# Attention and token selection on one core: ranking by half sections, the gate's exp moved, one group's q scaled through TensorE

## The chip, the cores and the metric

One core of a Trainium2 chip runs the whole program. The metric is the device time of one execution in microseconds (us). All arithmetic is float32. The engines are TensorE (PE; its weight loads are shown as PEld), VectorE (DVE), ScalarE (ACT) and GpSimd (POOL); SyncE (SP) only issues DMAs.

## What is computed

Eight batches of twelve heads go through attention (448 positions, 64 columns per head) with normalized q and k. Its result, 448 tokens of 768 columns per batch, then goes through a layer that only the 128 best tokens of a batch get:

```python
q_n, k_n = rmsnorm(q, g_q), rmsnorm(k, g_k)        # x / sqrt(mean(x*x) + 1e-6) * g
attn = softmax(q_n @ k_n.T / sqrt(64))
x = concat_heads(attn @ v)                         # (8, 448, 768)
scores = x @ w_gate                                # one number per token
top = the 128 tokens of a batch with the highest scores
x[top] += sigmoid(scores[top]) * (relu(x[top] @ w1) @ w2)    # 768 -> 1024 -> 768
```

## The kernel before, in words

**Units and groups.** Four heads of a batch make a group, so there are 24 groups, three to a batch. A group has seven units, one for each 64 keys: 168 units. `scores(u)` (L265) multiplies one block of keys with all queries into two of the four score banks (pool `ps_sc`), and ACT's Exp turns them into probabilities `p` (seven buffers). `values(u)` multiplies `p` with v, `add_probs(u)` sums the probabilities on DVE. After a group's seventh unit, `values_out`, `sum_keys`, `invert_sums` and `to_tokens` (twice) bring the result into the token rows `x` of the batch, divided by the softmax sums.

**Normalization.** For each group, tokens are loaded (`load_tok`), squared on ACT (`squares`), summed on DVE and raised to -1/2 on POOL (`sum_squares`, L201). The factors of k go into the Exp as its scale. Those of q must lie along the free axis: `rows_out` writes them to DRAM, `rows_in` reads them back spread over the partitions (`bc`), and `scale_q` (L235) multiplies q by them on DVE. For group 0 alone `scale_q_early` (L239) does the same without DRAM: 28 small matmuls (the trace shows each matmul as two) in two score banks, and two multiplications on DVE.

**Ranking and selection.** When a batch's third group is done, `gate` gives the scores (DVE), `spread` copies them along the free axis, `score_rows` transposes them on PE and copies the result out on ACT, `count` compares each score with all others (four DVE instructions, L431), `annotate` makes the rank, the sigmoid (an Exp on ACT, L452, and six small DVE instructions) and the row number, `select` scatters the chosen rows into a DRAM buffer by four indirect DMAs on POOL (L464), and `load_selected` (L482, SP queue) reads them back. `mixture` is the two layers for the 128 rows: six transposes (L498), then eight pieces of PE work.

**Order.** It is written out by hand, each engine runs its instructions in that order, and semaphores are the only waits. The loop at the end (L698) goes by sections `q` of four units: scores and values of the units, then two half sections. A half section runs the actions whose slot it is (`at(slot, ...)`; a slot is a unit number, so section q has the slots 4q to 4q+3), one piece of a `mixture` (`piece`), and one waiting task (`opening(q, place)`, place 0 before the halves, 1 and 2 after the first and the second). `tasks` is a first-in first-out list, and only its first entry is looked at. `last_tokens` (L620) puts `gate`, `store_x` and `spread` into the next section and `ranks_of` as a task after it; `ranks_of` (L633) puts `count`, `annotate` and `select` into the section after that, and `load_selected` five slots behind `select`. `ready[b]` is the first section in which `mixture(b)` may begin, and `first_ff(b)` its lower bound. After the last unit (section 42) the loop goes on until the last batches are through. `mixture` works in one bank (`moe`), and only the last batch's uses the score banks (`bank()`, L511). A helper tile `aux` has one bank too, or the `moe` bank where no mixture is running.

Of the kernel before, what the change touches and what calls it, by code (L numbers as in the profile page):

```python
# [26 lines left out]
def fast(  # L27
# [25 lines left out]
    nc = tc.nc  # L53
# [52 lines left out]
    def load_q(n):  # L106
        c = n % NG * 2
        load("qT", qTs, qT[n // NG, c : c + 2].rearrange("c p s -> p c s"), [128, 2, S], n, 3)
# [10 lines left out]
    load_tok(0, 0)  # L119
    load_tok(0, 1)  # L120
    load_q(0)
    load_k(0)
    load_tok(1, 0)
    load_tok(1, 1)
    load_v(0)
    load_q(1)
# [250 lines left out]

    gates, rowss, highers, ranks, slots_dram = {}, {}, {}, {}, {}  # L380

    def store_x(b):
        nc.sync.dma_start(
# [21 lines left out]
    def spread(b):  # L405
# [5 lines left out]
        nc.vector.tensor_copy(out=t, in_=sc[:, :, None].to_broadcast([CP, NJ, CP]))  # L411
        rowss[b] = t

    def score_rows(b):
        t = rowss[b]
        ps = aux([128, 512], "row_ps")
        for j in range(NJ):
            nc.tensor.transpose(
                out=ps[:CP, CP * j : CP * (j + 1)], in_=t[:, j, :], identity=ident[:CP, :CP]
            )  # L420
        rows = moe_pool.tile([CP, S], F32, name="score_rows")
        nc.scalar.copy(out=rows, in_=ps[:CP, 0:S])
        rowss[b] = rows

    def count(b, js):
# [14 lines left out]

    def annotate(b):

        sc, x = gates.pop(b), xs[b]
        ranks[b] = moe_pool.tile([CP, NJ], I32, name="rank", bufs=2)
        nc.vector.tensor_copy(out=ranks[b], in_=highers.pop(b))

        parts = moe_pool.tile([CP, 2, NJ], F32, name="parts")
        nc.vector.tensor_scalar_min(out=parts[:, 0], in0=sc, scalar1=0.0)
        nc.vector.tensor_scalar(
            out=parts[:, 1], in0=sc, scalar1=0.0, scalar2=-1.0, op0=OP.max, op1=OP.mult  # L450
        )
        nc.scalar.activation(out=parts, in_=parts, func=AF.Exp)  # L452
        nc.vector.tensor_add(out=parts[:, 1], in0=parts[:, 0], in1=parts[:, 1])
        nc.vector.reciprocal(out=parts[:, 1], in_=parts[:, 1])
        nc.vector.tensor_mul(out=x[:, :, DM], in0=parts[:, 0], in1=parts[:, 1])
        nc.vector.tensor_scalar_add(out=x[:, :, DM + 1], in0=token_f, scalar1=float(b * S))  # L456

    def select(b):
# [26 lines left out]
    def mixture(b):  # L485

        n = CAP
        xe = xes.pop(b)
        xeT = moe_pool.tile([128, NDC, 128], F32, name="xeT")
        half = NDC // 2  # L490
        for a in range(2):
            if a == 0:
                ps = ps_moe.tile([128, 512], F32, tag="moe", name="moe_ps")
            else:
                ps = aux([128, 512], "xeT_ps")
            for i in range(half):
                dc = half * a + i
                nc.tensor.transpose(  # L498
                    out=ps[:, 128 * i : 128 * i + n],
                    in_=xe[:n, 128 * dc : 128 * (dc + 1)],  # L500
                    identity=ident[:n, :n],
                )
            nc.scalar.copy(  # L503
                out=xeT[:, half * a : half * (a + 1), :n],
                in_=ps[:, : half * 128].rearrange("p (i t) -> p i t", t=128)[:, :, :n],
            )
        row = moe_pool.tile([128, 1], I32, name="row", bufs=2)
        nc.vector.tensor_copy(out=row[:n], in_=xe[:n, DM + 1 : DM + 2])
        yield False

        def bank():  # L511

            if b == B - 1:
                return ps_sc.tile([128, 512], F32, name="sc")
            return ps_moe.tile([128, 512], F32, tag="moe", name="moe_ps")

        hT = moe_pool.tile([128, NFC, 128], F32, name="hT")
        for f0 in range(0, NFC, 4):
            ps = bank()
            for i in range(4):  # L520
# [15 lines left out]
            yield True  # L536
        for a in range(2):
            cols = slice(DM // 2 * a, DM // 2 * (a + 1))
            ps = bank()
            for fc in range(NFC):  # L540
                nc.tensor.matmul(  # L541
                    out=ps[:n, : DM // 2],
                    lhsT=hT[:, fc, :n],
                    rhs=w2[:, fc, cols],
                    start=(fc == 0),
                    stop=(fc == NFC - 1),
                )
                if fc == NFC // 2 - 1:
                    yield False
            nc.vector.scalar_tensor_tensor(  # L550
                out=xe[:n, cols],
                in0=ps[:n, : DM // 2],
                scalar=xe[:n, DM : DM + 1],
                in1=xe[:n, cols],
                op0=OP.mult,
                op1=OP.add,
            )
            if a == 1:
                nc.gpsimd.indirect_dma_start(  # L559
                    out=out.flatten_outer_dims(),  # L560
                    out_offset=bass.IndirectOffsetOnAxis(ap=row[:n, :1], axis=0),
                    in_=xe[:n, 0:DM],
                    in_offset=None,
                )
            yield True
# [11 lines left out]
    def at(slot, fn, *args):  # L577
        todo.setdefault(slot, []).append(lambda: fn(*args))

    def task(when, fn, *args):  # L580
        tasks.append((when, lambda: fn(*args)))

    def opening(q, place):
        if tasks and tasks[0][0] <= (q, place):
            tasks.pop(0)[1]()

    def prepare(n, slot):
        sq = {}
# [6 lines left out]
    for n in range(1, n_groups):  # L595
        s0 = NI * n
        if n > 2:
            at(max(s0 - 24, 0), load_tok, n, 0)
            at(max(s0 - 24, 0), load_tok, n, 1)
        at(max(s0 - 4, 3), scale_q, n)  # L600
        if n > 1:
            prepare(n, max(s0 - 16, 0))
            at(max(s0 - 13, 2), load_q, n)
            at(max(s0 - 11, 2), load_k, n)
            at(max(s0 - 11, 2), load_v, n)
# [9 lines left out]
        task((q + 1, 0), to_tokens, n, 0)  # L615
        task((q + 1, 1), last_tokens, n)

    now = [0]

    def last_tokens(n):  # L620
        to_tokens(n, 1)
        b, g = divmod(n, NG)
        q = now[0]

        s = PER * (q + 1) if n < n_groups - 1 else -9
        at(s, gate, n)
        if g < NG - 1:
            return
        at(s, store_x, b)
        at(s + 1, spread, b)  # L630
        task((q + 1, 1) if n < n_groups - 1 else (q + 1, 0), ranks_of, b)

    def ranks_of(b):  # L633
        score_rows(b)
        s = PER * (now[0] + 1) if b < B - 1 else -9
        at(s, count, b, (0, 1))
        at(s + 1, count, b, (2, 3))
        at(s + 2, annotate, b)
        at(s + 2, select, b)
        at(s + 7 if b < B - 1 else s + 3, load_selected, b)  # L640
        if b < B - 1:
            ready[b] = max(now[0] + 4, first_ff(b))
        else:
            ready[b] = 0

    def first_ff(b):


        return (units + 4 - NG * NI * (B - 2 - b)) // PER

    def run_values(upto, q):
        ended = False
# [10 lines left out]
            add_probs(u)  # L663

    sq = {}
    sq[0, 0] = squares(0, 0)
    sum_squares(0, 0, sq.pop((0, 0)))
    sq[0, 1] = squares(0, 1)
    sum_squares(0, 1, sq.pop((0, 1)))
    sq[1, 0] = squares(1, 0)  # L670
    sq[1, 1] = squares(1, 1)
    scale_q_early(0)
    sum_squares(1, 0, sq.pop((1, 0)))
    load_tok(2, 0)
    load_tok(2, 1)
    rows_out(1)
    sum_squares(1, 1, sq.pop((1, 1)))
    rows_in(1)

    def run(slots):  # L680
        for slot in sorted(x for x in todo if x < 0 or x in slots):
# [14 lines left out]
    waiting = list(range(units))  # L696
    moe, ready, done, q = iter(()), {}, 0, 0
    while done < B or tasks:  # L698
        now[0] = q
        k = PER * q  # L700
        for half in range(HALVES):
            for u in (k + 2 * half, k + 2 * half + 1):
                if u < units:
                    scores(u)
            run_values(k + 2 * half - 1, q)
        opening(q, 0)
        for half in range(HALVES):
            run((k + 2 * half, k + 2 * half + 1))
            end = piece(q)
            spare[0] = end is None and half == 0  # L710
            if end is not None or half == 0 or not ready:
                opening(q, half + 1)
            spare[0] = False
            run(())
        q += 1
# [531 lines left out]
```

## Time and profile before

| | |
|---|---|
| median of 3 runs | 570.66 us (570.5 to 572.22) |
| profiled execution | 572.16 us |
| its span | 570.4 us (1.76 us lie around it) |
| PE busy | 515.3 us, 90% |
| DVE busy | 354.7 us, 62% |
| ACT busy | 278.3 us, 49% |
| POOL busy | 196.6 us, 34% |
| mean granted PE clock | 0.972 |

Busy times are of the span. A granted clock of 1.00 is the 2.4 GHz level and 0.50 the 1.2 GHz level; a stretch in between is a mixture of both. The timeline view gives instructions in order of time, like ones merged, with the engine's idle time before them and what ended it.

### The profile page before, as it was taken

Reading aid. Unit: us, or ns where it says so; the run is one execution under the profiler, and the core shown is the slowest. Engines: PE = TensorE matmul, PEld = TensorE weight load, DVE = VectorE, ACT = ScalarE, POOL = GpSimd, SP = SyncE. Lnnn points to the kernel's source line nnn. Section 1 sums busy time; section 2 is a strip of 40 time slices with the busy share of each in tenths; the row PEclk is TensorE's granted clock in tenths of the full one; section 3 lists DMA queues with packets and bytes.
Section 4 is the critical chain, followed back from the end, with each engine's and each line's share of the span. In section 5 each row is a group of like instructions: output and inputs, shape, how many; then the busy total and the mean of one; then the engine's idle time right before and its main releaser. Section 6 shows DMA issues by size and latency. Waiting matters only on the chain. (4 is left out here: it accounts for less than half of the span.)

```text
span 570.4 us, 16312 instructions
## 1 busy us (share of the span) xinstructions
PE 515.3 (90%) x7028; PEld 288.5 (51%) x7028; DVE 354.7 (62%) x699; ACT 278.3 (49%) x506; POOL 196.6 (34%) x100
## 2 busy tenths in 40 slices
PE   6789787989997998999899999999999999929895
PEld 6334332347542456544664475446644665418482
DVE  2497887784768757578577556676596637472000
ACT  2757664665444755447464444474646454401010
POOL 3654643751232532173152332640354200130200
PEclk9979997999999899999999999999999999968999
DMA  6696889875762754619835682638816320012100
GB/s 227 206 305 197 290 240 346 289 234 173 224 217 75 214 167 166 194 31 271 269 81 174 191 243 83 163 117 247 219 52 186 99 99 2 30 58 96 56 29 32
DMA packets 47108, 94.02 MB, mean 165 GB/s; under 512 B 11702, under 2 KB 29878, under 8 KB 47028
## 3 DMA queue, kind: packets, MB, share of 16 engines
q1 hardware_dynamic: 43684, 86.58, 49.1%
q0 software_dynamic: 3200, 6.31, 3.2%
q8 instruction: 57, 0.93, 0.7%
q14 instruction: 23, 0.19, 0.1%
q10 hardware_dynamic: 144, 0.00, 0.0%
HBM read 75.39 MB, written 25.36 MB: 177 GB/s over the span
## 5 line engine op out<-in xcount | busy, mean ns | idle before, releaser
L285 ACT ACTIVATE p<-sc,rinv 128x448 f32<-128x448 f32 x336 | 186.2, 639 | 105.4 <-PE sc L276 87.3
L201 POOL TENSOR_TENSOR rinv<-ss,neg_half 128x14 f32<-128x14 f32 x48 | 142.9, 2981 | 218.3 <-issue 102.8
L276 PE MATMUL sc<-qT,kT 64*32 64x448 f32 x2688 | 155.4, 553 | 13.4 <-ACT p L285 7.1
L302 PE MATMUL av<-p,v 64*32 64x448 f32 x2688 | 151.6, 547 | 0.0
L315 DVE TENSOR_TENSOR sum<-sum,p 128x896 f32<-128x896 f32 x120 | 130.3, 1086 | 21.6 <-ACT p L285 14.1
L302 PEld LDWEIGHTS av<-p,v 64*32 64x32 f32 x2688 | 56.4, 109 | 74.3 <-issue 67.1
L276 PEld LDWEIGHTS sc<-qT,kT 64*32 64x32 f32 x2688 | 49.2, 108 | 85.8 <-issue 54.1
L522 PE MATMUL moe_ps<-xeT,w 128*128 128x128 f32 x672 | 80.7, 278 | 0.3 <-ACT hT L531 0.3
L522 PEld LDWEIGHTS moe_ps<-xeT,w 128*128 128x128 f32 x672 | 77.8, 194 | 3.7 <-issue 2.9
L541 PE MATMUL moe_ps<-w,hT 128*128 128x384 f32 x224 | 77.8, 492 | 1.4 <-DVE xe L550 0.7
L197 DVE TENSOR_REDUCE ss<-sq 128x14 f32<-128x896 f32 x48 | 51.8, 1078 | 11.3 <-ACT sq L191 10.9
L464 POOL DMA_INDIRECT selected<-x,rank x32 | 36.0, 1125 | 64.6 <-DVE x L456 56.7
L371 DVE TENSOR_TENSOR x<-x_ps,rden 112x512 f32<-112x512 f32 x48 | 32.8, 687 | 37.4 <-PE x_ps L369 37.2
L541 PEld LDWEIGHTS moe_ps<-w,hT 128*128 128x128 f32 x224 | 40.5, 190 | 30.1 <-issue 2.2
L191 ACT ACTIVATE sq<-tok 128x896 f32<-128x896 f32 x48 | 45.2, 962 | 5.8 <-DMA tok<-in_tok_dram 5.8
L395 DVE SCALAR_TENSOR_TENSOR prod<-x,wg 112x256 f32<-112x256 f32 x96 | 40.4, 421 | 2.5
L559 POOL DMA_INDIRECT out_dram<-xe,row x8 | 12.3, 1533 | 82.0 <-DVE rden L357 46.4
L531 ACT ACTIVATE hT<-moe_ps 128x512 f32<-128x512 f32 x14 | 8.4, 597 | 48.1 <-PE moe_ps L522 48.1
L357 DVE RECIPROCAL rden<-denT_ps 112x16 f32<-112x16 f32 x24 | 6.1, 254 | 40.1 <-PE denT_ps L355 40.0
L369 PEld LDWEIGHTS x_ps<-ident,xT 128*112 128x112 f32 x192 | 21.9, 137 | 17.8 <-issue 11.6
L369 PE MATMUL x_ps<-ident,xT 128*112 128x128 f32 x192 | 29.1, 284 | 2.0 <-ACT xeT L503 1.1
L550 DVE SCALAR_TENSOR_TENSOR xe<-moe_ps,xe 128x384 f32<-128x384 f32 x14 | 8.6, 616 | 35.6 <-PE moe_ps L541 35.6
(63 smaller groups left out, 281.3 us busy)
## 6 DMA issues: line engine op xcount, KB each, us to landing
tok<-in_tok_dram SPq DMA_DIRECT2D x48, 448.0 KB, 7.0
qT<-in_qT_dram SPq DMA_DIRECT2D x24, 448.0 KB, 5.7
kT<-in_kT_dram SPq DMA_DIRECT2D x24, 448.0 KB, 5.0
v<-in_vp_dram SPq DMA_DIRECT2D x24, 448.0 KB, 6.0
out_dram<-x SPq DMA_DIRECT2D x8, 1344.0 KB, 7.1
bc<-rows SPq DMA_DIRECT2D x46, 224.0 KB, 5.9
xe<-selected SPq DMA_DIRECT2D x8, 385.0 KB, 3.4
w<-in_moe_w_dram SPq DMA_DIRECT2D x6, 512.0 KB, 10.1
```

The source lines that it names most:

```text
L191: nc.scalar.activation(out=sq, in_=t, func=AF.Square, scale=scale)
L197: nc.vector.tensor_reduce(out=ss, in_=sq, axis=AX.X, op=OP.add)
L201: nc.gpsimd.tensor_tensor(out=rinv.rearrange(flat), in0=ss.rearrange(flat), in1=neg_half.to_broadcast([128, 2 * NI]), op=OP.pow,)
L276: nc.tensor.matmul(out=scs[hh][o : o + 32, 0:S], lhsT=kTs[n][r, c, D * i + k0 : D * i + k0 + 32], rhs=qTs[n][r, c, :], start=True, stop=True,)
L285: nc.scalar.activation(out=p[:, hh], in_=scs[hh][:, 0:S], func=AF.Exp, scale=rinvs[n, 1][:, hh, i : i + 1],)
L302: nc.tensor.matmul(out=avs[n][c][o : o + 32, 0:S], lhsT=vs[n][r, hh, i, d0 : d0 + 32], rhs=probs[u][r, hh], start=(i == 0), stop=(i == NI ...
L315: nc.vector.tensor_tensor(out=sums[n], in0=probs[u - 1] if i == 1 else sums[n], in1=probs[u], op=OP.add)
L369: nc.tensor.transpose(out=ps[:CP, j, :], in_=t[:, j, :], identity=ident)
L395: nc.vector.scalar_tensor_tensor(out=prod, in0=xs[b][:, j, cols], scalar=1.0, in1=wg[:, cols], op0=OP.mult, op1=OP.mult, accum_out=gates[b ...
L464: w = nc.gpsimd.indirect_dma_start(out=t[:, :], out_offset=bass.IndirectOffsetOnAxis(ap=rank[:, j : j + 1], axis=0), in_=x[:, j, :], in_of ...
L522: nc.tensor.matmul(out=ps[:, 128 * i : 128 * i + n], lhsT=w1[:, dc, 128 * (f0 + i) : 128 * (f0 + i + 1)], rhs=xeT[:, dc, :n], start=(dc == 0),
L541: nc.tensor.matmul(out=ps[:n, : DM // 2], lhsT=hT[:, fc, :n], rhs=w2[:, fc, cols], start=(fc == 0), stop=(fc == NFC - 1),)
```

## The change

Five things, and some order at the start:

- `last_tokens` and `ranks_of` put their actions into the current or next half section (`soon`) and no longer into the next section; `ranks_of` becomes the first of the tasks, `opening` looks at the first two, `load_selected` comes four slots behind `select`, and `ready` and `first_ff` move one section forward.
- The sigmoid's two inputs are made in `spread` and its Exp runs on ACT right behind the copy in `score_rows`; `annotate` keeps the three DVE instructions that follow.
- Group 1's q is scaled by `scale_q_early` too, as the first task of section 0, without `rows_out(1)` and `rows_in(1)`.
- `mixture` of any batch takes score banks from section 43 on.
- At the start `load_tok(1, 0)` is issued ahead of `load_k(0)`, and `sum_squares(1, 0)` comes ahead of `scale_q_early(0)`.

```diff
-    load_k(0)
     load_tok(1, 0)
+    load_k(0)
...
     def spread(b):
...
+        parts[b] = moe_pool.tile([CP, 2, NJ], F32, name="parts", bufs=2)
+        nc.vector.tensor_scalar_min(out=parts[b][:, 0], in0=sc, scalar1=0.0)
+        nc.vector.tensor_scalar(
+            out=parts[b][:, 1], in0=sc, scalar1=0.0, scalar2=-1.0, op0=OP.max, op1=OP.mult
+        )
     def score_rows(b):
...
         nc.scalar.copy(out=rows, in_=ps[:CP, 0:S])
+        nc.scalar.activation(out=parts[b], in_=parts[b], func=AF.Exp)
     def annotate(b):
-        parts = moe_pool.tile([CP, 2, NJ], F32, name="parts")
-        nc.vector.tensor_scalar_min(out=parts[:, 0], in0=sc, scalar1=0.0)
...
-        nc.scalar.activation(out=parts, in_=parts, func=AF.Exp)
...
         def bank():
-            if b == B - 1:
+            if PER * now[0] >= units + 2:
                 return ps_sc.tile([128, 512], F32, name="sc")
...
     def opening(q, place):
-        if tasks and tasks[0][0] <= (q, place):
-            tasks.pop(0)[1]()
+        now[:] = q, place
+        for i, (when, fn) in enumerate(tasks[:2]):
+            if when <= (q, place):
+                tasks.pop(i)
+                fn()
+                return
...
-        at(max(s0 - 4, 3), scale_q, n)
         if n > 1:
+            at(s0 - 4, scale_q, n)
...
+    def soon():
+        q, place = now
+        return PER * q + 2 * place if PER * q < units else -9
     def last_tokens(n):
         to_tokens(n, 1)
         b, g = divmod(n, NG)
-        q = now[0]
-        s = PER * (q + 1) if n < n_groups - 1 else -9
+        s = soon()
         at(s, gate, n)
         if g < NG - 1:
             return
         at(s, store_x, b)
         at(s + 1, spread, b)
-        task((q + 1, 1) if n < n_groups - 1 else (q + 1, 0), ranks_of, b)
+        q, place = now
+        tasks.insert(0, ((q, 2) if place == 0 else (q + 1, place - 1), lambda: ranks_of(b)))
     def ranks_of(b):
         score_rows(b)
-        s = PER * (now[0] + 1) if b < B - 1 else -9
+        s = soon()
         at(s, count, b, (0, 1))
         at(s + 1, count, b, (2, 3))
         at(s + 2, annotate, b)
         at(s + 2, select, b)
-        at(s + 7 if b < B - 1 else s + 3, load_selected, b)
-        if b < B - 1:
-            ready[b] = max(now[0] + 4, first_ff(b))
-        else:
-            ready[b] = 0
+        at(s + 6 if s >= 0 else s + 3, load_selected, b)
+        ready[b] = max((s + 6) // PER + 1, first_ff(b)) if b < B - 1 else 0
     def first_ff(b):
-        return (units + 4 - NG * NI * (B - 2 - b)) // PER
+        return (units - NG * NI * (B - 2 - b)) // PER
...
-    sq[1, 0] = squares(1, 0)
-    sq[1, 1] = squares(1, 1)
+    for key in ((0, 0), (0, 1), (1, 0), (1, 1)):
+        sq[key] = squares(*key)
+        if key != (1, 1):
+            sum_squares(*key, sq.pop(key))
     scale_q_early(0)
-    sum_squares(1, 0, sq.pop((1, 0)))
+    sum_squares(1, 1, sq.pop((1, 1)))
     load_tok(2, 0)
     load_tok(2, 1)
-    rows_out(1)
-    sum_squares(1, 1, sq.pop((1, 1)))
-    rows_in(1)
+    tasks.append(((0, 1), lambda: scale_q_early(1)))
```

## Rows read from the trace of the kernel before

**Rows 1.** Stretches: us, busy (x instructions) by engine, clock, DMA share, GB/s
```profile
20.00:60.00 40.00, 34.54 (x610) 14.69 (x590) 27.79 (x40) 27.56 (x49) 22.33 (x8) 0.91 0.64 200
60.00:100.00 40.00, 31.40 (x552) 12.72 (x552) 32.95 (x61) 24.00 (x43) 17.49 (x10) 0.91 0.95 312
300.00:400.00 100.00, 98.29 (x1322) 55.41 (x1321) 67.53 (x132) 51.58 (x95) 33.52 (x16) 1.00 0.60 173
500.00:515.00 15.00, 4.10 (x22) 2.97 (x23) 10.49 (x36) 1.41 (x4) 4.72 (x4) 0.63 0.28 95
```
**Rows 2.** Timeline of the first sections: start us, us, instruction, [idle before <-releaser]
```profile
13.68 1.67 PE L247 MATMUL sc<-ident,rinv 64*64 64x64 f32 x56
14.76 1.32 DVE L255 SCALAR_TENSOR_TENSOR qT<-qT,gg,sc 128x448 f32<-128x448 f32 x2 [3.47 <-PE sc L247]
...
22.68 1.09 DVE L197 TENSOR_REDUCE ss<-sq 128x14 f32<-128x896 f32 x1 [2.14 <-ACT sq L191]
...
29.07 1.15 DVE L235 SCALAR_TENSOR_TENSOR qT<-qT,gg,bc 128x896 f32<-128x896 f32 x1 [5.10 <-DMA bc<-rows]
...
30.32 1.75 PE L276 MATMUL sc<-qT,kT 64*32 64x448 f32 x16 [4.62 <-issue]
...
31.79 3.27 PE L302 MATMUL av<-p,v 64*32 64x448 f32 x32
```
**Rows 3.** Timeline around the first batch's ranking
```profile
61.79 0.99 PE L276 MATMUL sc<-qT,kT 64*32 64x448 f32 x16 [1.55 <-ACT p L285]
...
88.30 0.99 PE L418 MATMUL row_ps<-ident,spread 112*112 112x112 f32 x4 [2.89 <-DVE spread L411]
...
89.22 3.24 PE L276 MATMUL sc<-qT,kT 64*32 64x448 f32 x32
```
**Rows 4.** Timeline around the second batch's ranking
```profile
183.85 0.21 ACT L452 ACTIVATE parts<-parts 112x8 f32<-112x8 f32 x1 [5.14 <-DVE parts L449]
...
185.47 3.32 PE L276 MATMUL sc<-qT,kT 64*32 64x448 f32 x32 [4.33 <-ACT p L285]
...
188.01 3.66 PE L302 MATMUL av<-p,v 64*32 64x448 f32 x48
```
**Rows 5.** Waits, PE and SP: what waited for what, us in total, times, longest
```profile
PE row_ps L418 <- DVE spread L411: 6.2, 3, 2.9
...
SPq L482 <- DMA selected<-x,rank: 86.8, 6, 47.1
```
**Rows 6.** Timeline from the last attention matmuls to the end
```profile
498.16 1.73 PE L302 MATMUL av<-p,v 64*32 64x448 f32 x32
...
511.04 0.34 SPq L482 DMA_DIRECT2D xe<-selected  x1
...
514.26 0.88 PE L498 MATMUL moe_ps<-ident,xe 128*128 128x128 f32 x3 [5.04 <-DMA xe<-selected]
...
523.32 0.68 DVE L431 SCALAR_TENSOR_TENSOR cmp<-score_rows,gate,earlier 112x448 f32<-112x448 f32 x1 [8.95 <-ACT score_rows L422]
...
527.37 0.17 DVE L456 TENSOR_SCALAR x<-token_f 112x4 f32<-112x4 f32 x1
...
529.23 5.43 PE L541 MATMUL moe_ps<-w,hT 128*128 128x384 f32 x16 [0.69 <-ACT hT L531]
...
534.40 0.33 SPq L482 DMA_DIRECT2D xe<-selected  x1
...
541.51 0.55 PE L498 MATMUL moe_ps<-ident,xe 128*128 128x128 f32 x3 [0.71 <-DVE row L508]
```
**Rows 7.** Costliest groups on POOL and DVE: busy, mean ns | idle before, releaser
```profile
L201 POOL TENSOR_TENSOR rinv<-ss,neg_half 128x14 f32<-128x14 f32 x48 | 142.9, 2981 | 218.3 <-issue 102.8
...
L315 DVE TENSOR_TENSOR sum<-sum,p 128x896 f32<-128x896 f32 x120 | 130.3, 1086 | 21.6 <-ACT p L285 14.1
...
L371 DVE TENSOR_TENSOR x<-x_ps,rden 112x512 f32<-112x512 f32 x48 | 32.8, 687 | 37.4 <-PE x_ps L369 37.2
...
L395 DVE SCALAR_TENSOR_TENSOR prod<-x,wg 112x256 f32<-112x256 f32 x96 | 40.4, 421 | 2.5
```

More of the change, by code (lines that the diff above doesn't have):

```diff
@@ L121, in fast @@
     load_q(0)
+    load_tok(1, 0)
     load_k(0)
-    load_tok(1, 0)
     load_tok(1, 1)
@@ L376, in to_tokens @@
         )
-    gates, rowss, highers, ranks, slots_dram = {}, {}, {}, {}, {}
+    gates, parts, rowss, highers, ranks, slots_dram = {}, {}, {}, {}, {}, {}
     def store_x(b):
@@ L441, in annotate @@
     def annotate(b):
-        sc, x = gates.pop(b), xs[b]
+        x, p = xs[b], parts.pop(b)
+        gates.pop(b)
         ranks[b] = moe_pool.tile([CP, NJ], I32, name="rank", bufs=2)
         nc.vector.tensor_copy(out=ranks[b], in_=highers.pop(b))
-        parts = moe_pool.tile([CP, 2, NJ], F32, name="parts")
-        nc.vector.tensor_scalar_min(out=parts[:, 0], in0=sc, scalar1=0.0)
-        nc.vector.tensor_scalar(
-            out=parts[:, 1], in0=sc, scalar1=0.0, scalar2=-1.0, op0=OP.max, op1=OP.mult
-        )
-        nc.scalar.activation(out=parts, in_=parts, func=AF.Exp)
-        nc.vector.tensor_add(out=parts[:, 1], in0=parts[:, 0], in1=parts[:, 1])
-        nc.vector.reciprocal(out=parts[:, 1], in_=parts[:, 1])
-        nc.vector.tensor_mul(out=x[:, :, DM], in0=parts[:, 0], in1=parts[:, 1])
+        nc.vector.tensor_add(out=p[:, 1], in0=p[:, 0], in1=p[:, 1])
+        nc.vector.reciprocal(out=p[:, 1], in_=p[:, 1])
+        nc.vector.tensor_mul(out=x[:, :, DM], in0=p[:, 0], in1=p[:, 1])
         nc.vector.tensor_scalar_add(out=x[:, :, DM + 1], in0=token_f, scalar1=float(b * S))
@@ L578, in at @@
         todo.setdefault(slot, []).append(lambda: fn(*args))
+    now = [0, 0]
     def task(when, fn, *args):
@@ L616, in finish @@
         task((q + 1, 1), last_tokens, n)
-    now = [0]
+    def soon():
+        q, place = now
+        return PER * q + 2 * place if PER * q < units else -9
     def last_tokens(n):
@@ L665, in fast @@
     sq = {}
[L666 to L669, printed above, removed]
-    sq[1, 0] = squares(1, 0)
-    sq[1, 1] = squares(1, 1)
+    for key in ((0, 0), (0, 1), (1, 0), (1, 1)):
+        sq[key] = squares(*key)
+        if key != (1, 1):
+            sum_squares(*key, sq.pop(key))
     scale_q_early(0)
-    sum_squares(1, 0, sq.pop((1, 0)))
+    sum_squares(1, 1, sq.pop((1, 1)))
     load_tok(2, 0)
     load_tok(2, 1)
-    rows_out(1)
-    sum_squares(1, 1, sq.pop((1, 1)))
-    rows_in(1)
+    tasks.append(((0, 1), lambda: scale_q_early(1)))
     def run(slots):
@@ L698, in fast @@
     while done < B or tasks:
-        now[0] = q
+        now[:] = q, 0
         k = PER * q
```

## The prediction

> **What bounds the kernel now.** I read the stretches first. From 300 to 400 us PE is busy for 98 of 100 us at full clock: there TensorE is the bound and other engines cost nothing. From 20 to 100 us it is idle for 14 of 80 us at clock 0.91, while DVE fills 33 of the 40 us from 60 on; and from 500 to 515 us PE works for 4.1 of 15 us [rows 1]. So time can only come from PE's idle stretches and from what runs at half clock behind them. The timeline and the waits name them. (a) PE idles 4.62 us before 30.32: the next scores need group 1's q, whose scaling on DVE waited 5.10 us for `bc` from DRAM [rows 2]. (b) 1.55 us at 61.79 and 2.89 us at 88.30, where the transposes of the score row wait for `spread` [rows 3]. (c) 4.33 us before 185.47: the Exp of batch 1's sigmoid waits 5.14 us on ACT, because DVE must finish four `count`s first, and the Exps of the probabilities stand behind it [rows 4]. (d) The wait of the row transposes on `spread` comes three times, 6.2 us in all, 2.9 of them in (b) [rows 5]. (e) The end: the last values end at 498.16 + 1.73 = 499.89, and PE gets the selected rows of batch 6 at 514.26, those of batch 7 at 541.51 [rows 6]. Half clock is seen in the rows: 32 value matmuls take 1.73 us at full clock and 3.27 after (a) [rows 2, 6]; 32 score matmuls, of the same size (64x448), take 3.24 and 3.32 after the waits of 2.89 and 4.33 us [rows 3, 4]. A unit's scores are 16 of them and its values 16, so a unit is 1.73.
>
> **The change part by part.**
>
> *Group 1's q through the array.* Two writes and two reads of DRAM go from SP's queue, with SP's waits for them, so the loads behind them start earlier. Added are 1.67 us on PE and 1.32 us on DVE for 1.15 us [rows 2]. The new DVE work stands behind `sum_squares(2,0)`: 22.68 + 1.09 + 0.17 (its small addition, an estimate from the same kind of row) = 23.9, so it ends near 25.3, and the sixth unit's scores wait for its two banks. Before, PE was through with four more half units at 30.32 - 4.62 = 25.70, so it would now be there at about 25.70 - 4 x 0.87 + 1.67 = 23.9: a new wait of 1.4 us. Removed: 4.62 us idle, and at half clock 1.75 - 0.87 and 3.27 - 1.73, or 2.4 us. Net 7.0 - 1.7 - 1.4 = 3.9; some half clock ran on after these rows, so I take 4.5. Bounds: 0, if DVE takes it all back in the next sections, and 7.
>
> *Load order and `sum_squares(1,0)` at the start.* DVE now sums group 1's squares ahead of group 0's q scaling (14.76). The tile comes one load earlier, for which about 1.2 us is an estimate from 448 KB at the rate of these loads; its sum then ends close to 14.9. I take 0, with bounds of -1 and +0.5.
>
> *First batch's ranking, gate of group 0.* `gate(0)` moves from ahead of `scale_q(3)` into the section before, which takes the 1.55 us at 61.79; the row transposes now come a section's matmuls after `spread`, which takes 2.89 us and the half clock behind it (3.24 - 1.73, and as much again for the next 32). At most 1.55 + 2.89 + 3.0 = 7.4. But here DVE is close to its own limit. Section 6 now has on DVE four additions (4 x 1.09), two `x` (2 x 0.69), one q scaling (1.15), a sum of squares (1.27), a gate (4 x 0.47 with the accumulator's read) and `spread` with the two small ones (0.8): 10.8 us. Section 7 has 4.3 + four counts 2.9 + 1.27 + 0.8 + 1.15 = 10.4 [rows 2, 6, 7]. PE needs about 8 us for each (4 units at 1.73, and 1 of transposes). So DVE decides, and its work is not less than before, only closer packed. I take 4, bounds 0 and 7.4.
>
> *The Exp of the sigmoid behind the score row.* Its inputs are ready since `spread`, so ACT no longer waits for the counts. In the second batch 4.33 us idle and (3.32 - 1.73) + (3.66 - 1.5 x 1.73) = 2.7 us of half clock go, 7.0. Its ranking falls into sections 12 and 13 now, which hold pieces of batch 0's layers, so PE has work of its own while DVE counts. I take 6.5; bounds 0 (the same block of counts stalls the `p` buffers elsewhere) and 7.
>
> *Row transposes behind `spread` in the other batches.* 6.2 - 2.9 = 3.3 us [rows 5]. Batches 1 and 5 keep a piece of a layer between the two, as some did before without a wait. I take 3, bounds 0 and 3.3.
>
> *The end.* Batch 6's last tokens are done in section 38. Before, its gate came in 39, its row in 40, its counts in 41, and its layers in 44, after all attention. Now gate and `spread` come in 38, row, counts and `select` in 39, `load_selected` in 40, and the bound lets the layers start in 42, right behind the last values. The same PE work stands ahead of 499.89, so I count from there, in the new order. Six transposes of batch 6's rows (0.55 for three [rows 6]), four of tokens and the den sums (0.6 each), with one short wait for the shared bank: to +2.9. First half of the first layer, 5.4 (16 x 384 columns took 5.43 [rows 6]; 48 x 128 took the same): +8.3. Token transposes of group 23, half a layer piece of 2.7 between them: +12.9. DVE: `x` 0.7, gate 1.9, reduce and `spread` 0.6: +16.2. Transposes, copy and counts: before, from the first count at 523.32 to the end of L456 at 527.54 it was 4.2, of which the Exp's turn of 0.3 goes; with 1.2 for transposes and copy (PE is through with them at +16.8): +21.2. From there to the load's issue 534.40 - 527.54 = 6.9, and from issue to PE 514.26 - 511.04 = 3.2 [rows 6]: +31.3. PE ends batch 6's second layer at 16.8 + 2 x 5.4 = +27.7 and then waits 3.6 us. Batch 7's layers started at 541.51 - 499.89 = +41.6 before: 10.3 us earlier. The wait is longer than the 2.89 us after which the clock halved [rows 3], so I take off 2.5, about what the waits above cost: 7.8, say 8. Bounds: 3, if each of batch 7's steps waits for a whole piece more, and 10.3. The free banks are in this sum: PE writes the next half while the last is read out.
>
> The Trainium skill, "TensorE: Matmul & The Clock Gate", section "Why this matters for your kernels", says that a wait of PE between bursts of matmuls brings the clock back to half, and so speaks against this part of the change, which leaves PE one such wait. The waits of 2.89 to 4.62 us here agree; after the one of 1.55 us the matmuls ran at full clock. By the rule the end gives 8 us, and with the clock held it would give 10.3 and a time of 544.5.
>
> *Smaller things.* `store_x` and `select` go one to two sections forward on SP and POOL; the loads ahead of them are two groups early, which hides that. `load_selected` comes a slot earlier behind `select`, in SP's queue ahead of loads of later groups (a rival, below).
>
> Sum: 4.5 + 4 + 6.5 + 3 + 8 = 26. For waits that the new order makes I take off 2, about one more wait of the kind in (b): 24. The profiled execution took 572.16 us, 1.5 over the median, so 572.16 - 24 = 548 there, and 547 against the median of 570.66.
>
> **The rivals.**
> 1. *DVE holds the opening.* The first ten sections are bound by DVE's work, which does not shrink, so group 1's lead and the first ranking give 2 us of 8.5. For: 33 of 40 us busy from 60 to 100 us. Against: DVE idled 12 us from 20 to 60 us, 5.1 of them in the wait that goes [rows 1, 2]. Time 547 + 6.5 = 553.5.
> 2. *The count block only moves.* Parts (c) and (d) stall PE in other sections, and 9.5 us do not come: 556.5. Against: these sections now have layer pieces.
> 3. *SP's queue, slower than before.* `load_selected` reaches the head of SP's queue before its rows have landed. From the last DVE instruction to the issue took 6.9 us with POOL free [rows 6]; a `pow` ahead of `select` on POOL adds 3.0 [rows 7], and a section without layers lasts about 7: SP stands for some 3 us, and the loads of q, k, tokens and `bc` behind it come late. That decides once such a stand exceeds the loads' lead. Then seven batches at 3 us, each with 2.5 us of half clock, cost 38 against the sum's 24: 585. Against: SP waited 86.8 us at this very place, once 47.1 us [rows 5], and none of PE's waits above is its effect.
> 4. *It gives more.* All idle and half-clock time listed goes, and the clock holds at the end: 7 + 7.4 + 7 + 3.3 + 10.3 = 35: 536.
> 5. *The end doesn't get shorter*, because every step of batch 7's ranking stands behind a layer piece on PE: 5 us less, 552.
>
> **How the numbers follow.** Forecast 0.55, rivals 0.2, 0.07, 0.04, 0.08 and 0.06. The forecast's own range is 541 to 552, the others stretch it to 537 and 559. What differs by less than 0.3% (1.7 us) can't be told from no change here; between the cases and that lies only rival 3 and an unnamed mixture of losses, 0.04: faster 0.92, same 0.03, slower 0.05.
>
> **What would show it.** No wait of 4 us on PE near 26 to 30 us, and scores of group 1 at full clock; no 5 us wait of the sigmoid's Exp on ACT; no wait of row transposes near 80 us; transposes of batch 6's rows within 3 us of the last values, and of batch 7's some 31 us after them, at half clock. The forecast is wrong if DVE is busy over 95% from 30 to 100 us with PE waiting as much as before, if L482 on SP is followed by late q or k, or if the layers of batch 6 start before the last values or well after them.

## The result and the profile after

| | before | changed |
|---|---|---|
| median, us (runs) | 571.44 (570.50 to 573.75, 4) | 554.32 (548.22 to 556.10, 4) |
| profiled execution, us (span) | 572.16 (570.4) | 548.22 (546.5) |
| TensorE's granted clock, span's mean | 0.972 | 0.991 |
| PE's waits in the span, warm-up left out, us | 43.2 | 27.1 |

The ratio is 0.9676 (95% interval 0.9592 to 0.976): faster, as forecast, by 17 us in the median and by 23.9 us between the profiled executions. The profiled execution of the changed kernel is the best of its four, so the rows below show the change at its best; the others have spans of 551.2, 554.0 and 554.4 us at clocks of 0.982, 0.977 and 0.976. That spread is a finding of its own, below.

The same stretches as in [rows 1], and two of 5 us (window, us, busy of PE, PEld, DVE, ACT, POOL with instructions, PE clock, DMA share, GB/s):

```profile
20.00:60.00 40.00, 37.33 (x723) 17.35 (x715) 30.04 (x46) 29.34 (x52) 22.31 (x13) 1.00 0.75 222
60.00:100.00 40.00, 34.58 (x648) 14.78 (x640) 37.39 (x72) 28.47 (x53) 20.55 (x9) 1.00 0.90 310
...
500.00:515.00 15.00, 11.50 (x42) 6.75 (x40) 5.86 (x23) 1.24 (x3) 4.71 (x5) 1.00 0.43 131
300.00:305.00 5.00, 4.33 (x27) 3.97 (x28) 2.73 (x11) 0.96 (x3) 4.65 (x2) 0.66 0.03 1
515.00:520.00 5.00, 3.71 (x17) 3.33 (x18) 0.15 (x1) 0.96 (x2) 0.00 (x0) 0.66 0.30 118
```

The opening runs at full clock (0.91 before), and from 500 us PE works for 11.5 of 15 us (4.1 before). What is to be seen against rival 1: from 60 to 100 us DVE is busy for 37.4 of 40 us, close to its limit, and PE gains all the same. In slices of 5 us the clock was below 0.9 before at 30, 35, 85, 90, 185 and 505 to 515 us; now it is so at 300, 515 and 540 only (540, like 565 before, lies in the last us, where PE hardly works). The place at 300 is new.

PE's waits and SP's wait for the selected rows, after (what waits, for what: us in total, times, longest):

```profile
PE sc L276 <- issue: 5.0, 3, 2.4
PE moe_ps L499 <- DMA xe<-selected: 4.1, 1, 4.1
PE x_ps L369 <- ACT xeT L504: 3.4, 4, 1.5
PE den_ps L337 <- ACT xeT L504: 2.5, 3, 1.4
...
PE row_ps L424 <- DVE parts L416: 0.7, 1, 0.7
...
SPq L483 <- DMA selected<-x,rank: 97.0, 8, 21.4
```

The row transposes' wait for `spread`, 6.2 us in three [rows 5], is down to 0.7. New at the head are waits for `xeT`: the second half of a batch's row transposes uses the one shared auxiliary bank, and `den_ps` and `x_ps` stand in line for it until ACT has copied it out, 5.9 us in seven waits. Before, these two waited 2.3 us for it, in four.

The opening's landmarks, after (timeline: start us, us, instruction, [idle before <-releaser]). L325 reads out a group's finished values, here of groups 0, 3 and 4:

```profile
13.15 1.68 PE L247 MATMUL sc<-ident,rinv 64*64 64x64 f32 x56
...
21.38 1.67 PE L247 MATMUL sc<-ident,rinv 64*64 64x64 f32 x56
...
23.35 1.27 DVE L255 SCALAR_TENSOR_TENSOR qT<-qT,gg,sc 128x448 f32<-128x448 f32 x2
...
33.81 1.01 ACT L325 COPY xT<-av 128x448 f32<-128x448 f32 x2
...
55.58 0.65 PE L369 MATMUL x_ps<-ident,xT 128*112 128x128 f32 x4 [1.68 <-DVE rden L357]
...
63.53 0.59 PE L337 MATMUL den_ps<-sum,pick_pair 128*32 128x224 f32 x8 [1.88 <-DVE sum L315]
...
74.41 0.99 PE L276 MATMUL sc<-qT,kT 64*32 64x448 f32 x16 [1.45 <-issue]
...
77.75 0.97 ACT L325 COPY xT<-av 128x448 f32<-128x448 f32 x2
...
94.02 0.98 ACT L325 COPY xT<-av 128x448 f32<-128x448 f32 x2
```

and the same read-outs before, which no row shows yet:

```profile
38.72 0.98 ACT L325 COPY xT<-av 128x448 f32<-128x448 f32 x2
...
82.51 0.97 ACT L325 COPY xT<-av 128x448 f32<-128x448 f32 x2
...
104.45 0.98 ACT L325 COPY xT<-av 128x448 f32<-128x448 f32 x2
```

The lead is 4.9 us at group 0, 4.8 at group 3 and 10.4 at group 4, behind the first ranking. From group 0 to group 3 it does not grow: PE's wait of 1.55 us at 61.79 [rows 3] is gone, but the two of 1.68 and 1.88 us above stand in its place. At the last values it is 499.89 - 484.40 = 15.5. The end adds 8.4: 23.9 in all.

The end, after, to be read against [rows 6]:

```profile
482.67 1.73 PE L302 MATMUL av<-p,v 64*32 64x448 f32 x32
...
484.82 0.49 PE L499 MATMUL moe_ps<-ident,xe 128*128 128x128 f32 x3
...
501.30 0.57 PE L424 MATMUL row_ps<-ident,spread 112*112 112x112 f32 x4 [0.70 <-DVE parts L416]
...
516.29 0.70 PE L499 MATMUL moe_ps<-ident,xe 128*128 128x128 f32 x3 [4.09 <-DMA xe<-selected]
...
517.61 12.09 PE L523 MATMUL sc<-xeT,w 128*128 128x128 f32 x96
```

Batch 6's transposes start right behind the last values, and its layers fill the time in which batch 7 is ranked. What is left is a wait of 4.09 us, with half clock at the start of the 96 matmuls behind it.

### The profile page after: what moved, and what is told of

Same layout as the page of the kernel before. It is cut to its first block, busy times and chain, and to the rows that moved or that the text cites. A ratio compares the mean times of both kernels' runs of the same rounds, so it can differ in the third digit from the quotient of the medians.

```text
span 546.5 us, 16420 instructions
## 1 busy us (share of the span) xinstructions
PE 507.3 (93%) x7084; PEld 288.3 (53%) x7084; DVE 356.1 (65%) x700; ACT 277.1 (51%) x506; POOL 188.2 (34%) x100
## 4 chain that ended last, share of the span: by engine, by line
PE 55%; issue 19%; ACT 3%; DVE 2%; POOL 1%; DMA 1%; POOLq 0%; DVEq 0%
PE sc L276 15%; PE av L302 13%; PE moe_ps L523 11%; PE moe_ps L542 10%; PE x_ps L369 3%; PE den_ps L337 1%; DVE sum L315 1%; POOL selected L465 1%; ACT p L285 1%; DMA out_dram<-xe,row 1%; ACT xeT L504 1%; PE denT_ps L355 1%; DVE ss L197 1%; ACT sq L191 1%; ACT xT L325 1%
## 5 line engine op out<-in xcount | busy, mean ns | idle before, releaser
L201 POOL TENSOR_TENSOR rinv<-ss,neg_half 128x14 f32<-128x14 f32 x48 | 140.0, 2919 | 221.0 <-DVE ss L198 120.4
L276 PE MATMUL sc<-qT,kT 64*32 64x448 f32 x2688 | 152.0, 540 | 7.1 <-issue 5.0
L302 PE MATMUL av<-p,v 64*32 64x448 f32 x2688 | 149.3, 536 | 0.0
L523 PE MATMUL moe_ps<-xeT,w 128*128 128x128 f32 x624 | 75.8, 280 | 0.0
L523 PEld LDWEIGHTS moe_ps<-xeT,w 128*128 128x128 f32 x624 | 73.1, 195 | 3.3 <-issue 3.3
L465 POOL DMA_INDIRECT selected<-x,rank x32 | 34.7, 1084 | 98.0 <-DVE x L457 90.3
L542 PE MATMUL moe_ps<-w,hT 128*128 128x384 f32 x192 | 66.4, 489 | 0.0
L542 PEld LDWEIGHTS moe_ps<-w,hT 128*128 128x128 f32 x192 | 34.6, 190 | 21.3 <-issue 2.2
L438 DVE SCALAR_TENSOR_TENSOR cmp<-score_rows,gate,earlier 112x448 f32<-112x448 f32 x32 | 21.9, 684 | 10.6 <-ACT score_rows L428 9.9
L315 DVE TENSOR_TENSOR sum<-p 128x896 f32<-128x896 f32 x24 | 26.0, 1082 | 3.6 <-ACT p L285 3.6
```

The lines of the kernel that those rows point to most:

```text
L201: nc.gpsimd.tensor_tensor(out=rinv.rearrange(flat), in0=ss.rearrange(flat), in1=neg_half.to_broadcast([128, 2 * NI]), op=OP.pow,)
L276: nc.tensor.matmul(out=scs[hh][o : o + 32, 0:S], lhsT=kTs[n][r, c, D * i + k0 : D * i + k0 + 32], rhs=qTs[n][r, c, :], start=True, stop=True,)
L302: nc.tensor.matmul(out=avs[n][c][o : o + 32, 0:S], lhsT=vs[n][r, hh, i, d0 : d0 + 32], rhs=probs[u][r, hh], start=(i == 0), stop=(i == NI ...
L315: nc.vector.tensor_tensor(out=sums[n], in0=probs[u - 1] if i == 1 else sums[n], in1=probs[u], op=OP.add)
L465: w = nc.gpsimd.indirect_dma_start(out=t[:, :], out_offset=bass.IndirectOffsetOnAxis(ap=rank[:, j : j + 1], axis=0), in_=x[:, j, :], in_of ...
L523: nc.tensor.matmul(out=ps[:, 128 * i : 128 * i + n], lhsT=w1[:, dc, 128 * (f0 + i) : 128 * (f0 + i + 1)], rhs=xeT[:, dc, :n], start=(dc == 0),
```

## The experiments

Each kernel's edit is against the changed kernel unless it says "on before". Times are medians; each ratio is to the kernel before as run on the same chip.

**The changed kernel again, as it is**, to see what sets its spread.

> The changed kernel once more, for the spread of its runs. Theory: its runs differ by stretches at half clock alone, so span and mean granted clock move together: 0.991 stands with a span of 546.5 us, and each 0.01 of clock less costs about 5.5 us (0.976 with 554). Rival: the spread is in DMA or start times; then runs at the same clock differ by several us.

552.15 us (548.15 to 555.87, six runs), ratio 0.963 (0.9586 to 0.9674). Spans and clocks: 546.3 at 0.991, 546.7 at 0.991, 549.6 at 0.988, 551.3 and 551.4 at 0.982, 554.2 at 0.977. So 0.014 of clock goes with 7.9 us, 5.6 us for each 0.01, about 1% of the span, and runs at one clock lie within 0.4 us: the spread goes with the clock. Two of its places are to be seen in the profiled one (551.3 us), where the program's waits are those of the run above:

```profile
231.68 3.23 PE L276 MATMUL sc<-qT,kT 64*32 64x448 f32 x32 [2.40 <-issue]
...
490.17 7.25 PE L523 MATMUL moe_ps<-xeT,w 128*128 128x128 f32 x48
```

and in the faster run (546.5 us) of the same program:

```profile
230.91 1.74 PE L276 MATMUL sc<-qT,kT 64*32 64x448 f32 x32 [2.40 <-issue]
...
487.95 5.62 PE L523 MATMUL moe_ps<-xeT,w 128*128 128x128 f32 x48
```

The same wait, 2.40 us, with half clock behind it in one execution and without in the other: 1.5 us. These two places make 3.1 of the 4.8 us between the two spans, and a start that is 0.8 us later another part (the first L247 begins at 13.93, not 13.15). The slower executions, up to 554.4 us, have no trace, so where their half clock lies is not shown.

**Group 1's q through the array, and the start's order with it** (on before).

```
+ for key in ((0, 0), (0, 1), (1, 0), (1, 1)):   # sum_squares(1, 0) ahead of group 0's q
...
- rows_out(1); rows_in(1)
+ tasks.append(((0, 1), lambda: scale_q_early(1)))
```

> The kernel before with group 1's q through the array and the new order at the start alone. Theory: the lead of 4.9 us at the first group's end is kept to the end, ratio 0.991 to 0.993. Rival, DVE holds the opening: the lead is gone by the first layers, ratio over 0.996.

568.45 us, ratio 0.9926 (0.99 to 0.9952): 4.3 us less than before. The array without the start's order was not run.

**The start's order alone** (on before): the loop over the keys and the tokens' load ahead of k's, with group 1's factors still through DRAM.

```
+ for key in ((0, 0), (0, 1), (1, 0), (1, 1)):
+     sq[key] = squares(*key)
+     if key != (1, 1):
+         sum_squares(*key, sq.pop(key))
...
  rows_out(1); rows_in(1)
```

> The kernel before with the new order at its start alone (tokens of group 1 loaded and summed ahead), group 1's q still through DRAM. Theory after the run without the array, where the first group ended at 35.2 us against 34.0: the order gives about 3.5 of the 4.9 us at the first group's end and the array the rest; PE's wait for bc falls from 4.6 to about 2.9 us, time 2 to 4 us less. Rival: only the array takes that wait away; the first group ends near 38.7 us and the time stays within 1 us.

570.35 us, ratio 0.9954 (0.9932 to 0.9976), 1.7 us by the medians and 2.6 by the ratio. Its opening:

```profile
13.81 1.67 PE L247 MATMUL sc<-ident,rinv 64*64 64x64 f32 x56
...
17.82 1.39 SPq L214 DMA_DIRECT2D rows<-rinv  x2
...
28.48 0.99 PE L276 MATMUL sc<-qT,kT 64*32 64x448 f32 x16 [2.64 <-issue]
...
29.23 2.81 PE L302 MATMUL av<-p,v 64*32 64x448 f32 x32
...
35.60 0.98 ACT L325 COPY xT<-av 128x448 f32<-128x448 f32 x2
```

and that of the kernel with the array:

```profile
14.63 1.67 PE L247 MATMUL sc<-ident,rinv 64*64 64x64 f32 x56
...
35.29 1.02 ACT L325 COPY xT<-av 128x448 f32<-128x448 f32 x2
```

Before, group 1's factors left for DRAM later:

```profile
19.98 1.35 SPq L214 DMA_DIRECT2D rows<-rinv  x2
```

The start itself wanders by 1.5 us between runs (group 0's factors, the first L247, begin at 13.1 to 14.7), so I count from there to the read-out of group 0's values: 38.72 - 13.68 = 25.04 us before, 21.79 with the order alone, 20.66 with the array, and 20.66 in the changed kernel. The order alone gives 3.25, the array 1.13 on top, together 4.38. The rows say how: group 1's squares are summed earlier, so its factors leave for DRAM earlier (17.82, not 19.98) and come back earlier, and the wait before its scores is 2.64 us where it was 4.62 [rows 2]. With the shorter wait the scores run at full clock (0.99 for 16 against 1.75) and the values at 2.81 against 3.27. That is 2.0 + 0.8 + 0.5 = 3.3 us without any array. By the times the split is less sharp: 2.6 us by this ratio, 4.2 by that of the run with the array, and the two intervals overlap. How much the array would give without the order stays open.

**The end alone** (on before): batches 6 and 7 with the new ranking order, the Exp with the score row, and the free score banks.

```
- s = PER * (q + 1) if n < n_groups - 1 else -9
+ s = PER * (q + 1) if b < 6 else PER * q + 2 * place if PER * q < units else -9
...
- if b == B - 1:
+ if PER * now[0] >= units + 2:
```

> The kernel before with the ranking by half sections, the early Exp and the free banks for batches 6 and 7 alone. Theory: batch 7's layers start some 32 us after the last values where they started 41.6 us after them, and the time falls by 8 to 9 us, ratio 0.984 to 0.987. Rival: the gain came from earlier parts, ratio over 0.992.

565.33 us, ratio 0.9868 (0.9842 to 0.9894): 7.5 us less. Its own end is less smooth than that of the full change. On DVE the products of the gate stand ahead of the last two additions, which end at 503.14, and the den sums on PE start 0.15 us behind them, after a wait of 2.64 us (in the full change 0.57, for ACT), with half clock behind:

```profile
503.29 0.97 PE L337 MATMUL den_ps<-sum,pick_pair 128*32 128x224 f32 x8 [2.64 <-DVE row L517]
504.19 6.83 PE L531 MATMUL moe_ps<-xeT,w 128*128 128x128 f32 x48
...
533.96 0.86 PE L507 MATMUL moe_ps<-ident,xe 128*128 128x128 f32 x3 [4.34 <-DMA xe<-selected]
```

The last values end at 499.84, so batch 7's layers start at +34.1, where some +32 was expected and +31.9 is what the full change has.

**The sigmoid's Exp back behind the counts.**

```
- parts[b] = ...; nc.scalar.activation(out=parts[b], in_=parts[b], func=AF.Exp)   # with spread and row
+ nc.scalar.activation(out=p, in_=p, func=AF.Exp)                                 # in annotate
```

> The changed kernel with the sigmoid's two inputs and its Exp back in annotate. Theory that the Exp itself held ACT (part c): ACT waits about 3 to 5 us for DVE in each batch again, and the first and third batch's, which fall into sections without layers or next to them, cost PE 3 to 6 us in all: ratio to the kernel before higher by 0.005 to 0.01 than that of the unchanged new kernel. Rival, the half sections did it and the Exp's place doesn't matter: within 1 us of the unchanged new kernel.

556.89 us, ratio 0.971 (0.9674 to 0.9747), 4.7 us over the changed kernel as it is on the same chip; the two intervals just touch. ACT waits again:

```profile
ACT parts L452 <- DVE parts L449: 21.4, 8, 4.2
```

Compared at one clock the loss is smaller: 554.6 at 0.982 against 553.0 and 553.1. So some 1.5 us go with plain waits (28.1 us on PE in the span, against 26.6 and 27.1), and the rest with half clock. Whether the edit makes half clock more likely six runs don't settle: they have clocks of 0.976 to 0.989, the ten of the changed kernel as it is 0.976 to 0.991.

**Useless transposes in the last wait**, to hold the clock: 24 transposes of the identity into a free score bank, whose result nothing reads.

```
+ if b == B - 1:
+     fill = ps_sc.tile([128, 512], F32, name="sc")
+     for _ in range(24):
+         nc.tensor.transpose(out=fill[:, 0:128], in_=ident, identity=ident)
```

> The changed kernel with 24 matmuls of no use (transposes into a free score bank) where PE waits 4.1 us for the last batch's rows. Theory: the clock there is a matter of PE's work alone, so the wait stays (the last rows land 31 to 32 us after the last values), but the last layers run at full clock: 48 matmuls of their first half in 5.4 us instead of 6.5, time about 1.3 us less in all runs. Rival: what slows the last layers is not the clock but cold buffers or the rows' DMA; nothing changes.

551.95 us (548.03 to 555.93), ratio 0.9633 (0.9583 to 0.9683): the same as without.

```profile
515.01 2.78 PE L492 MATMUL sc<-ident 128*128 128x128 f32 x24
...
519.75 0.55 PE L503 MATMUL moe_ps<-ident,xe 128*128 128x128 f32 x3 [1.96 <-DMA xe<-selected]
...
520.92 10.98 PE L527 MATMUL sc<-xeT,w 128*128 128x128 f32 x96 [0.29 <-ACT xeT L508]
```

The clock holds: 96 matmuls in 10.98 us, not 12.09, and the best runs have 0.995. But from the last values (487.39) the transposes of batch 7's rows start at +32.4, not +31.9. So some 0.6 of the 1.1 us remain, less than the spread of six runs can show.

**q scaled two slots earlier**, against the 2.40 us wait near 231 us.

```
- at(s0 - 4, scale_q, n)
+ at(s0 - 6 if s0 % 4 < 2 else s0 - 4, scale_q, n)
```

> The changed kernel with q's scaling on DVE half a section earlier for the groups whose first unit is first or second in a section. Theory: PE's three waits of 1.2 to 2.4 us before scores (5.0 us in all) come from that DVE instruction standing behind a whole section's additions; they go, and with the one of 2.40 us goes the place near 231 us where the clock fell in one execution and not in another: 4 to 6 us less, and less spread. Rival: bc isn't there half a section earlier, DVE stands waiting for it, and the time stays or grows.

549.95 us (548.16 to 550.25), ratio 0.9586 (0.9558 to 0.9614), some 2 us less and not 4 to 6. The wait at 231 us is gone, and the spread is 2 us, but in the opening the earlier scaling stands on DVE ahead of what PE needs, and the clock falls there to 0.67 to 0.9 in five slices:

```profile
57.56 1.10 PE L369 MATMUL x_ps<-ident,xT 128*112 128x128 f32 x4 [2.75 <-DVE rden L357]
...
91.48 1.62 PE L276 MATMUL sc<-qT,kT 64*32 64x448 f32 x16 [2.22 <-ACT p L285]
```

There PE waited before the edit too, but for 1.9 us at most, and in the profiled execution at full clock. (In that of the next kernel, which scales q as the changed one does, a wait of 1.69 us near 56 us has half clock behind it: 32 score matmuls take 3.24 us, not 1.74.) Over the span PE's waits are 25.4 us, against 27.1: most of the wait has only moved.

**The second half of the row transposes in a score bank**, against the waits for the shared one.

```
- ps = aux([128, 512], "xeT_ps")
+ ps = ps_sc.tile([128, 512], F32, name="sc")
```

> The changed kernel with the second half of the selected rows' transposes in a score bank instead of the one shared with den, denT and x. Theory: the waits around that bank at the start of each mixture (x and den sums on ACT's copy 5.9 us, the transposes on x and rden 2.7 us in all) go, and with them the half clock near 300 us: 5 to 8 us less. Rival: the bank taken from the scores makes PE wait for an Exp instead, and the time stays.

541.92 us (541.65 to 544.95), ratio 0.9461 (0.9431 to 0.949), 10 us under the changed kernel's 552.15 on another chip, and as much under the 551.95 of the kernel with the useless transposes on this one. At one clock, 0.991, it is 541.8 against 548.2: 6.4 us. PE's waits fall from 27.1 to 21.7 us in the span; `den_ps` and `x_ps` wait for `xeT` no more, and the layers' start near 300 us, which was at half clock, is at full clock:

```profile
298.83 0.49 PE L499 MATMUL sc<-ident,xe 128*128 128x128 f32 x3
299.45 0.59 PE L337 MATMUL den_ps<-sum,pick_pair 128*32 128x224 f32 x8
301.02 5.62 PE L523 MATMUL moe_ps<-xeT,w 128*128 128x128 f32 x48 [0.99 <-ACT xeT L504]
```

where the changed kernel has

```profile
298.72 0.55 PE L499 MATMUL xeT_ps<-ident,xe 128*128 128x128 f32 x3 [0.46 <-DVE x L371]
300.67 0.59 PE L337 MATMUL den_ps<-sum,pick_pair 128*32 128x224 f32 x8 [1.40 <-ACT xeT L504]
301.18 7.25 PE L523 MATMUL moe_ps<-xeT,w 128*128 128x128 f32 x48
```

**All three of these**: the diffs of the fill, the earlier scaling and the bank together.

> The three edits of the other kernels of this call together. Theory: waits and half-clock places add, so 10 to 14 us less than the changed kernel, about 540 us, and a mean clock of 0.99 in most runs. Rival: what the one gives the other takes, about 546 us.

542.44 us (541.94 to 543.04), ratio 0.9462 (0.9436 to 0.9489): no better than the bank alone. PE waits for 17.2 us only, but the early scaling's half clock in the opening is there (0.68 to 0.89 in five slices), which by this trace takes what the shorter waits give.

The next three ran on a chip on which the kernel before took some 3% longer (590.13 us, at the same clocks), so their times compare only among themselves and with that.

**Free score banks for batch 7 alone**, as the kernel before had them.

```
- if PER * now[0] >= units + 2:
+ if b == B - 1:
```

> The changed kernel with batch 6's layers in the one moe bank to their end, as before. Theory: PE waits three times for ACT's or DVE's reading of that bank (0.3 to 1.4 us each, the fourth piece starts a new batch), 2 us in all, but batch 7's rows come no earlier, so PE's wait for them, 4.1 us, shrinks by the same: within 1 us of the unchanged new kernel. Rival: the banks carry part of the gain at the end: 2 us slower.

563.55 us, ratio 0.9576 (0.9542 to 0.961). The changed kernel as it is did not run on this chip, so its 0.963 from elsewhere settles little; the rows of the end do:

```profile
522.02 5.43 PE L542 MATMUL moe_ps<-w,hT 128*128 128x384 f32 x16 [0.71 <-DVE xe L551]
...
530.75 0.87 PE L499 MATMUL moe_ps<-ident,xe 128*128 128x128 f32 x3 [3.30 <-DMA xe<-selected]
```

Without the banks PE waits 0.71 us for one between two halves of the layer, and 3.30 us for batch 7's rows where it was 4.09. Counted from the last values (498.68) the rows come at +32.1 instead of +31.9. From there to the end of the span it is 62.5 us, with the banks 62.1. The wait for the rows ends last either way, so the banks are worth next to nothing here.

**The middle, with the start's new order**: batches 0 to 5 in the new order, the end and the way of group 1's q as before. The expectation left the start's order out, 2.6 us by its ratio.

```
- tasks.append(((0, 1), lambda: scale_q_early(1)))
+ rows_out(1); rows_in(1)
+ at(max(s0 - 4, 3), scale_q, n)
...
- s = soon()
+ s = soon() if b < 6 else PER * (now[0] + 1) if n < n_groups - 1 else -9
```

> The ranking by half sections and the early Exp for batches 0 to 5 alone; group 1's q goes through DRAM, batches 6 and 7 and the banks are as before. Theory: the parts add up; whole ratio 0.963, array part 0.9926, end part 0.9868, so this one 0.982 to 0.986, 8 to 10 us. Rival: the parts need each other (an opening held by DVE), ratio over 0.99.

570.73 us, ratio 0.9673 (0.9656 to 0.9691), 19.4 us under before on this chip, well more than expected. It is 7.2 us behind the kernel above, which has the end and the array too; these measured 7.5 and some 1 us on the other chips, so the order among the two fits, and it is the distance to before that is large on this chip. It is not used for the middle's size. On the chip of the first experiments the medians leave for the middle what the opening and the end don't take: 20.6 - 4.3 - 7.5 = 8.8 us.

**The bank, the transposes in the last wait, and the early scaling from group 9 on only.**

```
+ at(s0 - 6 if s0 % 4 < 2 and n > 8 else s0 - 4, scale_q, n)   # with the edits of the fill and of the bank
```

> The changed kernel with the transposes' own score bank, the 24 filling matmuls at the end, and q's scaling half a section earlier from group 9 on alone. Theory: the opening keeps the order in which bc is there in time, the wait of 2.4 us near 231 us is gone, and the last layers run at full clock: 536 to 540 us, 2 to 4 us under the kernel with all three edits. Rival: the spread of the opening's clock hides it, 541 to 543 us.

553.69 us (551.48 to 553.87), ratio 0.9368 (0.9348 to 0.9389), at a clock of 0.995 to 0.996; one slice of its profile is below 0.97. It beats the kernel before and, on the same chip, the changed one with batch 7's banks (563.55) by 9.9 us. Whether it beats the bank alone was not measured on one chip, and so its expectation in us is neither met nor refuted.

## Why the prediction came out as it did

It said 24 us for the profiled execution (548) and 547 for the median. The profiled execution took 548.22. The median is 554.32, inside the whole range (537 to 559) and 2.3 us outside the forecast's own (541 to 552). By its steps, measured between the two profiled executions:

| step | predicted, us | measured, us | from |
|---|---|---|---|
| group 1 through the array | 4.5 | 1.1 | opening, array against order alone |
| order of the start | 0 | 3.25 | opening, order alone |
| first ranking, gate of group 0 | 4 | 5.7 | lead at group 4 less that at group 3 |
| Exp, row transposes, less new waits | 6.5 + 3 - 2 = 7.5 | 5.1 | lead at the last values less that at group 4 |
| end | 8 | 8.4 | spans less the lead at the last values |
| sum | 24 | 23.5 | the other 0.4: a start 0.5 earlier by chance, less 0.1 lost from group 0 to 3 |

By medians it is less: 17.1 us here, and 20.6 on the chip of the first experiments, where the opening has 4.3, the end 7.5 and the middle the remaining 8.8. The profiled execution is the best of its four, and the steps' misses cancel (1.1 + 3.25 for 4.5; 1.7 more and 2.4 less), so that the total came out within 0.5 us is in part luck.

**The end: right.** From the last values, batch 7's transposes were to start at +31.3 and do at +31.9. Batch 6's second layer was to end at +27.7 and does at 512.20, +27.8. The wait was to be 3.6 us and is 4.09; half clock behind it costs 12.09 - 10.98 = 1.1 us, not 2.5. "The free banks are in this sum" credits them with what they don't give: without them the same rows come 0.2 us later.

**The opening: right sum, wrong owner.** The forecast gave 4.5 us to the array and "I take 0" to the start's order. The order alone does three quarters of it. The step that failed is the term put at 0: it prices the start's order by the sum's place on DVE alone, and leaves out that the trip through DRAM starts when these squares are summed, so that the order moves the trip and its wait too (4.62 to 2.64 us). The array's term took the whole wait for its own. The 1.4 us wait that was to come for group 1's q did not show: DVE began its scaling at 23.35, and PE has no wait from then to 38 us.

**The first ranking: low by 1.7.** The forecast took half of what was there because DVE looked like the limit. It is close to one (37.39 of 40 us busy from 60 to 100 us), but its work is packed closer, and the longest of PE's waits from 20 to 100 us is 1.88 us, all at full clock. All of the gain comes behind group 3; the gate of group 0, counted with 1.55 us, gave none, as DVE holds PE in other waits there. That much of rival 1 came true; its sum, 2 of 8.5 us, is refuted: the lead is 10.4 us at group 4.

**The middle: over-sized by 2.4.** The waits named went: none on the sigmoid's Exp, 0.7 of 6.2 us on `spread`. That the Exp's own place was worth 6.5 us does not show: putting it back, with the half sections kept, costs 4.7, and 1.5 at one clock. What came instead are waits for the shared bank and for q near 231 us, which rival 2's mechanism (another buffer's stall) had in general but not by name; its sum, all of this part lost, is refuted. Moving one use of the bank gives 6.4 us at one clock. Not all of that is the change's doing: PE's waits around this bank (of the den sums, of `x` and of the rows' transposes) were 4.9 us before and are 10.5 us after.

**The median: the step that it lacked.** The forecast counted half clock once, at the end. Behind waits of 0.5 to 2.4 us that the change leaves, the clock falls in some executions and not in others, and executions of one program spread over 8 us. The forecast's 547 is what the best ones come near (548.15 to 548.41); the one that was traced at 551.3 us has half clock at two more places, 3.1 us in all. That the median came near rival 1's 553.5 is chance: rival 1's mechanism is not what the rows show. With the 2.40 us wait moved, or the bank's waits gone, the spread is 2 to 3 us in five runs each.

The Trainium skill, "TensorE: Matmul & The Clock Gate", section "Why this matters for your kernels", says that a long gap between bursts of matmuls brings the clock back to half. The wait of 4.09 us agrees (0.66 from 515 to 520 us), and the filled one too (10.98 us for 96 matmuls). The section limits its rule to long gaps, and the wait of 2.40 us, behind which the clock fell in one execution and not in another, is not one of these: there the runs alone speak.

**Rivals 3 to 5.** SP waited 97.0 us for the selected rows, more than before, and no wait of PE or DVE for a load of q, k or `bc` follows from it. Rival 5 had the end no shorter; it is, by 8.4. Rival 4's 536 was not reached.

## What to carry to other kernels

When two edits meet at one wait, price each by the chain that ends it: the trip of `bc` began with the sum of squares, so an earlier sum alone gave 3.25 of the 4.4 us that a new path through the array was credited with. Once the large waits are gone, look for a helper buffer that several steps share; here moving one use of a single bank gave 6.4 us at one clock, more than the whole opening. Give a kernel's time with the granted clock of each run: a few short waits, behind which the clock falls in some executions only, make a spread of 1.4%, and a best run is not a median.

## What the hardware showed that was not expected

- The same program, at the same wait of 2.40 us, went on at full clock in one execution (32 matmuls in 1.74 us) and at half in another (3.23 us).
- Half clock also came after short waits alone: in the changed kernel's profiled execution 0.46 and 1.40 us, with transposes between them, and then 0.66 from 300 to 305 us.
- Transposes alone kept the clock: with 24 of the identity as the only work in 4.6 us before batch 7's rows, the 96 matmuls behind took 10.98 us, not 12.09.
- On one chip the kernel before took 3% longer at the same mean clock (590 against 572 us), and the kernels compared there were slow too. The profile of one shows stretches of a few us where value matmuls lie further apart at a granted clock of 1.00. Here the 16 that take 0.99 us elsewhere last from 222.09 to 225.30, with batch 7's banks alone:

```profile
222.09 2.01 PE L302 MATMUL av<-p,v 64*32 64x448 f32 x10
224.28 1.02 PE L302 MATMUL av<-p,v 64*32 64x448 f32 x6 [0.18 <-issue]
```

  What stretches them no run here settles.
